# One written list of operations, engines and PSUM banks in place of a planner with priorities

## The chip, the cores and the metric

The kernel runs on one core of one Trainium2 chip. The metric is the device time of one execution in microseconds (us). Three runs of the kernel before took 1002.0, 1002.21 and 1002.55 us; the median, 1002.21, is its time.

## What is computed

Three stages follow one another. The first is a linear attention with a delta rule over 4 x 8 heads, 768 steps, head size 48; the other two are two-layer MLPs with 384 -> 2048 -> 384 features over the 3072 tokens that result.

```python
for t in range(S):                       # attention, k normalised first
    y[:, :, t] = einsum('bhd,bhde->bhe', q[:, :, t], state)
    v_old = einsum('bhde,bhd->bhe', state, k_n[:, :, t])
    state = state + beta_t * outer(k_t, v_t - v_old)
x = y.transpose(0, 2, 1, 3).reshape(3072, 384)
h = x @ w_in                             # first MLP
x = where(h >= 1, h, where(h <= -1, 0, (h + 1)**2 / 4)) @ w_out
h = x @ w_in2                            # second MLP
out = (h * clip(h + 3, 0, 6) / 6) @ w_out2
```

## The kernel before

**Attention in chunks.** The 768 steps are cut into 12 chunks of 64, named c0 to c11. For each chunk k and q are loaded and transposed (lines 904 to 922), the norms of k are worked out (`norms`, L862), the products k k and k q are formed on PE (`products`, L932), read out of PSUM and masked (L956, L964, L978). `inverse` (L993) then solves a triangular system. Its inner part is a chain of pairs, a multiplication (L1019) and a subtraction (L1024), each of which needs the one before; chunks c0 and c1 do it on DVE, c2 and later ones on POOL. DVE prepares it (L1040, L1046, L1048) and transposes the result (L1057, L1058), and small tiled matmuls on PE finish it. `chain` (L1123) subtracts the old values from V (L1137), multiplies by the solved matrix, forms the new state, and `chain_y` (L1174) writes the output as the MLP's input XB (L1245).

**MLPs.** Each fp32 product is made of three faster ones, from a high part and a low remainder of either operand. So every weight tile f (16 of 128 hidden columns per MLP) is loaded into RAWL or RAWR and split by `wload` (L1266): bit operations (L1303, L1306, L1309), a rounded copy for the high part (L715, L718), and a subtraction for the low part (L707). H means the first product, O the second; H1 b0 f3 is the first product of MLP 1, block 0, tile 3. Blocks 0 and 1 are one chunk each (256 tokens), the others two. A group of such a product is three matmuls. Between H and O the activation runs on ACT and DVE (L1372 to L1374), its result is split the same way (GH, GL). The second MLP starts when the attention and the first one are through.

**Who sets the order.** The functions above don't issue anything. They register operations in a `Plan` (`op`, L300): what it reads and writes, which engines may run it (`alts`, with an assumed duration for each) and a priority. `emit` (L331) then simulates all engines on the host, step by step, with these durations, priorities per kind and chunk (`PR`), a model of the clock and of PE's instruction fetch, and chooses each operation's engine, place and PSUM bank. While PE would have nothing to do it puts in a filler, a dummy matmul whose result nobody reads (`fill`, L1657), to keep the clock up; there are 40 of them, without dependence or on a converted weight. After that `rearrange` (L580) puts single operations elsewhere by a table `MOVES` and sets some engines by a table `TAKEN`, and `run` (L601) calls the functions in the final order. Each engine executes its own instructions in that order, and semaphores are set between them.

```python
        self.order = order
        self.rearrange()
        self.run()
```

Nearly all matmuls come from one helper line, L749; L707, L715, L718, L720 and L723 are helper lines as well (two-operand pass; copies on POOL, on ACT and on DVE; scaled copy on DVE). L771, L773 and L778 are the scalings by a per-partition factor.

Of the kernel before, what the change touches and what calls it, by code (L numbers as in the profile page):

```python
# [17 lines left out]
TAIL = dict(pe=235, dve=125, act=130, pool=45)  # L18
MLP = 50
RATIO = 0.649  # L20
NSMALL = 2
WINDOW = 4096 / 1.2
WARM, COLD = 0.39, 0.49
PR = dict(tl=67.962086, tp=0.420514, pk=1,
          pg={(0, 'chain'): -0.2539, (0, 'inv'): 3.364608, (0, 'kv'): 1.465035, (0, 'lv'): -4.010662, (0, 'norm'): -0.274261, (0, 'sv'): 1.013448,
# [5 lines left out]
              (2, 'chain'): -0.290685, (2, 'inv'): -0.035632, (2, 'kv'): 0.669398, (2, 'lv'): -2.096759, (2, 'norm'): -0.160388,  # L31
# [10 lines left out]
              (9, 'norm'): 0.012878, (9, 'pm'): -0.418629, (9, 'tok'): -0.040633, (9, 'y'): 1.271522}, dx=1.008178, sx=39.637984, dl=760.706049,  # L42
          ms=('act', 'dve'), wd=4, fm=9792.35537, aw=('act', 'dve', 'pool'), mg=8, fl=4694.34542, off=(-10.25393, 8.909221, -35.984542, -41.02295),
          mb=(80.821727, -28.998599), slots=2, fast=(0,), slate=0, mk=0, hm=-109.564616, kv=-31.465847, tok=-1.884445, norm=17.151989, tr=-1.768853,
          prod=-34.319006, pm=-5.471625, inv=-15.779498, sv=25.627625, w=-1.449, chain=8.008585, y=3.551141, wl=12.667074, wls=0.825794,
          mp=-10.624354, lv=-23.102311, first=-4.800254, bias=-1265.49322, fill=3000, tpool=(2, 3, 4, 5, 6, 7, 8, 9, 10, 11), hc=1, halves=1,
          biasa=1240.32542, b16=(0, 1, 2, 3), hyst=2858.41045, fgap=480.938837, me=100, c3=('act', 'dve'), back=2155.50193, dh=200,
          margin=845.586248, umargin=89.653885, urg=('inv', 's', 'u', 'y'), sw=(217, 95), ad=('act', 'dve'), dp=('dve', 'pool'), ct=4,
          dg=('dve', 'pool'), dw=('dve', 'pool'), pq=190)

MOVES = ((12, -1), (17, 1), (11, 17), (20, 21), (0, 20), (55, 4), (82, 55), (2, 38), (6, 2), (7, 6), (5, 39), (81, 5), (56, 19), (8, 41), (9, 8),
# [224 lines left out]
class Bank:  # L276
# [8 lines left out]
    def free(self, e):  # L285
        return 0.0 if self.last[0] in (None, e) else self.last[1]


class Plan:

# [316 lines left out]
def fused_kernel(  # L607
# [19 lines left out]
    CH = 64  # L627
# [1082 lines left out]
```

## Time and profile before

| | |
|---|---|
| Time, median of 3 runs | 1002.21 us (1002.0 to 1002.55) |
| Profiled execution, first to last instruction (span) | 1004.1 us |
| Its distance from the median | 1.9 us |
| Instructions | 27311 |
| PE busy | 967.3 us, 96% |
| DVE busy | 610.3 us, 61% |
| ACT busy | 480.9 us, 48% |
| POOL busy | 295.5 us, 29% |
| Chain that ended last, share of PE | 86% |

The page gives no other time of the profiled execution than its span, from the first to the last instruction, so the span stands for it.

A busy share is a mean over the whole span, and this kernel has parts with different limits: in the page's 40 slices PE is busy for 6 to 8 tenths in the first four and for 9 or more in nearly all others. A row of the view by stretches shows for each engine how long it was busy and how many instructions it ran, then the granted clock of PE as a share of the full one and the busy share of the DMA engines. A row of the groups has the line, the engine, the operation, the tiles (out<-in), the shapes and the count, then the busy time of all, the mean of one in ns, and the idle time before them. DVE's neighbouring instructions overlap by some hundredths of a us, so a sum of their durations can exceed the time that they cover.

### The profile page before, as it was taken

How to read it: one execution, taken by the hardware profiler on the slowest of the kernel's cores; microseconds unless marked ns; L12 is line 12 of the kernel's file. 1: busy time of each engine (PE TensorE's matmuls, PEld its weight loads, DVE VectorE, ACT ScalarE, POOL GpSimd, SP SyncE). 2: the span in 40 equal slices, each digit the busy share in tenths (PEclk: the TensorE clock that was granted, in tenths of full speed). 3: DMA queues.
4: the chain of work that ended last, by engine and by line, in shares of the span. 5: the costliest groups of instructions: out<-in, count | busy, mean ns of one | idle time of the engine just before them, and what ended most of it. 6: DMA issues, size and time to landing. Idle time of an engine off the chain costs nothing.

```text
span 1004.1 us, 27311 instructions
## 1 busy us (share of the span) xinstructions
PE 967.3 (96%) x11543; PEld 835.6 (83%) x11543; DVE 610.3 (61%) x1136; ACT 480.9 (48%) x897; POOL 295.5 (29%) x649
## 2 busy tenths in 40 slices
PE   6778799999999999999999999999999999999998
PEld 4667699878778787787887888998989898999998
DVE  5898798777887688777546886225242324242421
ACT  4877565556564564545445774224242323232422
POOL 2101641767558565585710222110000000000000
PEclk9678999999999999999999999999999999999999
DMA  8872442443333234222213664002200200200000
GB/s 158 202 199 63 112 91 42 91 71 56 52 86 58 34 59 100 33 45 73 80 42 94 211 206 138 13 1 84 74 32 1 64 32 16 66 14 1 32 2 31
DMA packets 208459, 71.77 MB, mean 71 GB/s; under 512 B 154960, under 2 KB 204240, under 8 KB 208336
## 3 DMA queue, kind: packets, MB, share of 16 engines
q1 hardware_dynamic: 205376, 69.44, 28.9%
q8 instruction: 90, 1.47, 0.6%
q10 hardware_dynamic: 2960, 0.59, 0.3%
q14 instruction: 33, 0.27, 0.1%
HBM read 53.68 MB, written 14.16 MB: 68 GB/s over the span
## 4 chain that ended last, share of the span: by engine, by line
PE 86%; DVE 2%; POOL 1%; ACT 1%; issue 0%; POOLq 0%
PE bank L749 86%; POOL TMP L1019 1%; POOL TL L1024 1%; DVE GF L1374 0%; ACT GF L1373 0%; ACT GF L1372 0%; DVE LT L778 0%; DVE X L956 0%; DVE KQ L978 0%; ACT GH L718 0%; DVE DL L1040 0%; DVE DL L1057 0%; DVE E L1137 0%; DVE SM L874 0%; ACT X L771 0%
## 5 line engine op out<-in xcount | busy, mean ns | idle before, releaser
L749 PE MATMUL bank<-XB,WLA 128*128 128x512 f32 (+1 forms) x1404 | 325.6, 379 | 2.9 <-DVE GF L1374 2.8
L749 PEld LDWEIGHTS bank<-XB,WLA 128*128 128x128 f32 x1404 | 249.9, 190 | 51.2 <-DVE GF L1374 6.0
L1378 DVE SCALAR_TENSOR_TENSOR GF<-GF,bank 128x512 f32<-128x512 f32 x96 | 65.7, 687 | 161.7 <-ACT GF L1377 161.7
L1377 ACT ACTIVATE GF<-bank 128x512 f32<-128x512 f32 x96 | 57.0, 598 | 166.3 <-PE bank L749 156.8
L1019 POOL TENSOR_TENSOR TMP<-TL,DL 128x126 f32<-128x126 f32 (+25 forms) x278 | 115.3, 415 | 62.5 <-DVE DL L1077 35.5
L749 PE MATMUL bank<-GH,WLA 128*128 128x512 f32 (+1 forms) x504 | 120.9, 367 | 0.2 <-ACT XB L718 0.2
L1024 POOL TENSOR_TENSOR TL<-TL,TMP 128x126 f32<-128x126 f32 (+25 forms) x278 | 113.3, 407 | 21.8
L749 PE MATMUL bank<-XB,WLB 128*128 128x512 f32 (+1 forms) x468 | 108.7, 377 | 0.0
L718 ACT ACTIVATE GH<-GF 128x512 fp32r<-128x512 f32 x106 | 66.7, 630 | 81.7 <-DVE GF L1374 30.8
L707 DVE TENSOR_TENSOR GL<-GF,GH 128x512 fp32r<-128x512 f32 x105 | 77.6, 739 | 35.6 <-ACT GH L718 26.5
L749 PEld LDWEIGHTS bank<-GH,WLA 128*128 128x128 f32 x504 | 86.4, 190 | 15.2 <-ACT XB L718 0.4
L749 PEld LDWEIGHTS bank<-XB,WLB 128*128 128x128 f32 x468 | 82.9, 188 | 15.5 <-DVE GF L1374 0.4
L1372 ACT ACTIVATE GF<-bank 128x512 f32<-128x512 f32 x96 | 56.9, 593 | 73.6 <-PE bank L749 69.1
L1374 DVE SCALAR_TENSOR_TENSOR GF<-bank,GF 128x512 f32<-128x512 f32 x96 | 65.7, 685 | 36.5 <-ACT GF L1373 35.9
L749 PE MATMUL bank<-GL,WLA 128*128 128x512 f32 (+1 forms) x252 | 64.8, 366 | 0.0
L1373 ACT ACTIVATE GF<-GF 128x512 f32<-128x512 f32 x96 | 60.5, 630 | 2.5
L749 PEld LDWEIGHTS bank<-GL,WLA 128*128 128x128 f32 x252 | 43.9, 190 | 7.4
L749 PE MATMUL bank<-WLA,GH 128*128 128x384 f32 x205 | 43.4, 350 | 0.0
L707 POOL TENSOR_TENSOR GL<-GF,GH 128x512 fp32r<-128x512 f32 x15 | 20.2, 1344 | 72.4 <-ACT GH L718 48.9
L749 PE MATMUL bank<-GH,WLB 128*128 128x512 f32 (+1 forms) x168 | 39.4, 362 | 0.0
L749 PEld LDWEIGHTS bank<-WLA,GH 128*128 128x128 f32 x205 | 38.0, 196 | 1.5
L964 ACT ACTIVATE KQ<-bank 64x256 f32<-64x256 f32 (+1 forms) x72 | 27.2, 380 | 21.9 <-PE bank L749 17.1
(197 smaller groups left out, 1440.7 us busy)
## 6 DMA issues: line engine op xcount, KB each, us to landing
XB<-X SPq DMA_DIRECT2D x36, 256.0 KB, 4.6
X<-XB SPq DMA_DIRECT2D x30, 256.0 KB, 2.6
KQ<-in_moe_w_out_dram SPq DMA_DIRECT2D x16, 384.0 KB, 4.2
KQ<-in_moe_w_in_dram SPq DMA_DIRECT2D x16, 384.0 KB, 4.5
KN<-in_k_dram SPq DMA_DIRECT2D x24, 192.0 KB, 3.9
RAWL<-in_moe_w_out_dram SPq DMA_DIRECT2D x12, 384.0 KB, 4.5
out_dram<-E SPq DMA_DIRECT2D x24, 192.0 KB, 1.9
RAWL<-in_moe_w_in_dram SPq DMA_DIRECT2D x24, 144.0 KB, 4.3
```

What stands on the lines that cost most here:

```text
L707: alts[e] = (d, lambda e=e: ENG[e].tensor_tensor(out=val(out), in0=val(in0), in1=val(in1), op=op))
L718: lambda: nc.scalar.activation(out=val(out), in_=val(in_), func=AF.Copy, scale=scale))
L749: nc.tensor.matmul(o, l, r, start=start, stop=stop, skip_group_check=skip)
L964: alts = {"act": (285, lambda o=o, pin=pin: nc.scalar.activation(out=o, in_=pin(), func=AF.Copy, scale=1.0))}
L1019: P.op(te, d, lambda t=t, s=s, r0=r0, a0=a0, a1=a1, m=m: ve.tensor_tensor(out=t[:, a0:a1], in0=TL[:, r0 + a0:r0 + a1, s:s + 1].to_broadcas ...
L1024: P.op(te, d, lambda t=t, s=s, r0=r0, a0=a0, a1=a1: ve.tensor_tensor(out=TL[:, r0 + a0:r0 + a1, 0:s], in0=TL[:, r0 + a0:r0 + a1, 0:s], in1 ...
L1372: P.op("act", da, lambda: nc.scalar.activation(out=gf, in_=ps, func=AF.Relu, scale=0.5, bias=0.5), r=hkeys(hb, hv), w=gk, prio=mp)
L1373: P.op("act", da + 48, lambda: nc.scalar.activation(out=gf, in_=gf, func=AF.Square), w=gk, r=gk, prio=mp)
L1374: P.op("dve", 1.06 * n + 60, lambda: nc.vector.scalar_tensor_tensor(out=gf, in0=ps, scalar=1.0, in1=gf, op0=ALU.max, op1=ALU.min), r=hkeys ...
L1377: P.op("act", da, lambda: nc.scalar.activation(out=gf, in_=ps, func=AF.Relu, scale=1.0 / 6.0, bias=0.5), r=hkeys(hb, hv), w=gk, prio=mp)
L1378: P.op("dve", 1.06 * n + 60, lambda: nc.vector.scalar_tensor_tensor(out=gf, in0=gf, scalar=1.0, in1=ps, op0=ALU.min, op1=ALU.mult), r=hkey ...
```

## The change

The planner goes: `emit`, `rearrange`, the tables `PR`, `MOVES` and `TAKEN`, all priorities, and the bookkeeping of banks. A text `ORDER` takes their place, with one word for each of the 4625 operations and each filler. `1005p` would be operation 1005 on POOL (a ACT, d DVE, p POOL, n none), `403b25` an operation that gets PSUM banks 2 and 5, `f` a filler, `f1.0` one that reads a converted weight. The new `run` goes through it, refuses an operation ahead of what it depends on, and calls the functions. Operations are numbered in the order of registration, which is the same in both.

```diff
+ORDER = """
...
+"""
...
-    def emit(self, banks, spare, fill):
...
-    def rearrange(self):
...
+    def run(self, banks, fill):
+        done = set()
+        for x in ORDER.split():
+            if x[0] == "f":
+                fill(tuple(map(int, x[1:].split("."))) if x[1:] else None)
+                continue
+            n, e, bs = re.fullmatch(r"(\d+)([adpn]?)(?:b(\d+))?", x).groups()
+            i = int(n)
+            o = self.ops[i]
+            if not o["deps"] <= done:
+                raise ValueError(f"operation {i} before {sorted(o['deps'] - done)}")
+            done.add(i)
+            for b, j in zip(o["alloc"], bs or ()):
+                b.tile = banks[int(j)]
             if o["dyn"] is not None:
                 o["alts"] = o["dyn"]()
...
+            if e:
+                o["eng"] = dict(a="act", d="dve", p="pool", n="none")[e]
+            o["alts"][o["eng"]][1]()
+        assert len(done) == len(self.ops)
...
-        P.emit(banks[5:8], banks[0:5], fill)
+        P.run(banks, fill)
```

Set side by side with the order that the planner before arrives at, the list has the same operations, and these differences:

- 83 operations run on another engine: 32 go from DVE to POOL, 23 from ACT to DVE, 13 from DVE to ACT, 8 from ACT to POOL, 3 each from POOL to ACT and to DVE, and one mask (409) is no instruction any more, since its read-out, now on DVE, multiplies by the mask itself. From DVE to POOL go the low parts of weight tiles f0 to f11 (L707), the masks of c0 to c3 (L978), scalings of V (L707) and low parts of activations; from ACT to POOL go the rounded copies of f4 to f9 and of two single pieces.
- 8 fillers are left of 40, all ahead of the product that makes c0's new state.
- Within PE 66 operations, within DVE and ACT 88 each, within SP 92 and within POOL 14 stand elsewhere relative to the others. Chunk 0's loads of v are issued after the first weight tiles instead of before; the loads of q for c3 later; on ACT's queue the mask and beta go ahead of the identity. In the products of c0 the second half comes before the first. The norms of c1 are mixed into c0's solve.
- The banks come from all eight from the start, where the planner gave the front banks 5 to 7 first.
- Behind H1 b1 f5 on PE (141.22 us in the profile before), and behind places between 138.4 and 141.3 us on the other engines, the order of every engine is the same in both.

## Rows read from the trace of the kernel before

**Rows 1.** The page: the span, and each engine's busy time.
```profile
span 1004.1 us, 27311 instructions
...
PE 967.3 (96%) x11543; PEld 835.6 (83%) x11543; DVE 610.3 (61%) x1136; ACT 480.9 (48%) x897; POOL 295.5 (29%) x649
```

**Rows 2.** Busy time by stretches: engine (instructions), clock share, DMA share, GB/s.
```profile
8.00:101.00 93.00, 73.46 (x1625) 63.12 (x1623) 81.37 (x217) 66.90 (x132) 11.71 (x17) 0.80 0.66 155
101.00:126.00 25.00, 18.94 (x601) 17.48 (x601) 19.14 (x35) 13.19 (x23) 15.70 (x34) 1.00 0.48 116
126.00:545.00 419.00, 417.61 (x7038) 343.62 (x7038) 321.75 (x608) 233.31 (x475) 237.00 (x561) 1.00 0.32 64
```

**Rows 3.** The chain that ended last: start us, us, what.
```profile
101.36 0.23 POOL TMP L1019
...
115.33 0.24 POOL TL L1024
...
125.94 52.43 PE bank L749 x1162
...
545.11 455.60 PE bank L749 x2268
```

**Rows 4.** DVE's groups by line and shape from 8 to 101 us.
```profile
L707 DVE TENSOR_TENSOR WLA<-RAWL,WLA 128x768 fp32r<-128x768 f32 x8 | 7.6, 950 | 0.0
L978 DVE TENSOR_TENSOR KQ<-KQ,MSK 128x256 f32<-128x256 f32 x12 | 4.9, 412 | 3.0 <-ACT KQ L964 3.0
...
L707 DVE TENSOR_TENSOR WLA<-RAWL,WLA 128x384 fp32r<-128x384 f32 x6 | 3.7, 621 | 1.2 <-ACT WLA L718 1.2
...
L1054 DVE TENSOR_SCALAR TL<-TL,PAR 128x256 f32<-128x256 f32 x4 | 1.4, 352 | 0.1
...
L720 DVE COPY KQ<-bank 112x512 f32<-112x512 f32 x2 | 1.4, 688 | 0.0
...
L707 DVE TENSOR_TENSOR E<-E,NT 128x384 f32<-128x384 f32 x2 | 1.1, 550 | 0.0
```

**Rows 5.** POOL's groups by line and shape from 8 to 135 us.
```profile
L707 POOL TENSOR_TENSOR WLA<-RAWL,WLA 128x384 fp32r<-128x384 f32 x2 | 2.1, 1039 | 9.4 <-ACT WLA L718 9.3
L715 POOL CAST WLA<-RAWL 128x768 fp32r<-128x768 f32 x2 | 1.9, 947 | 3.4 <-DVE RAWL L1309 3.4
L707 POOL TENSOR_TENSOR WLB<-RAWR,WLB 128x768 fp32r<-128x768 f32 x1 | 1.9, 1852 | 2.7 <-ACT WLB L718 2.7
```

**Rows 6.** DVE's groups from 551 to 587 us, where POOL splits weights too.
```profile
L707 DVE TENSOR_TENSOR WLA<-KQ,WLA 128x768 fp32r<-128x768 f32 x7 | 7.8, 1114 | 0.1
```

**Rows 7.** POOL in order of time from 550 to 590 us: start, us, what.
```profile
582.72 2.58 POOL L707 TENSOR_TENSOR WLA<-KQ,WLA 128x768 fp32r<-128x768 f32 x1
```

**Rows 8.** PE in order of time, several stretches: start, us, what [idle before <-releaser].
```profile
25.72 5.03 PE L749 MATMUL bank<-GH 128*128 128x512 f32 x14
...
39.77 1.11 PE L749 MATMUL bank<-DL,NH 32*32 32x32 f32 x65
...
88.60 1.48 PE L749 MATMUL bank<-XB,WLA 128*128 128x256 f32 x6
...
114.94 2.35 PE L749 MATMUL bank<-XB,WLA 128*128 128x256 f32 x18
119.07 1.30 PE L749 MATMUL bank<-NH,LT 32*32 32x32 f32 x128 [1.79 <-DVE NH L1058]
```

**Rows 9.** Busy time by stretches of 20 us.
```profile
40.00:60.00 20.00, 16.11 (x501) 13.46 (x491) 18.11 (x48) 17.46 (x38) 4.07 (x5) 0.59 0.68 179
60.00:80.00 20.00, 15.83 (x267) 14.60 (x268) 19.56 (x49) 16.11 (x24) 0.66 (x2) 0.83 0.95 239
```

**Rows 10.** SP's issues in order of time from 56 to 80 us.
```profile
63.04 2.24 SPq L1286 DMA_DIRECT2D RAWL<-in_moe_w_in_dram  x3
```

**Rows 11.** DMA issues from 0 to 100 us: count, KB each, median us to landing.
```profile
RAWL<-in_moe_w_in_dram SPq DMA_DIRECT2D x24, 144.0 KB, 4.3
```

**Rows 12.** DVE in order of time from 62 to 72 us.
```profile
71.91 0.56 DVE L1303 TENSOR_SCALAR TBS<-RAWL 128x768 int32<-128x768 int32 x1
```

More of the change, by code (lines that the diff above doesn't have):

```diff
@@ L316, in op @@
         alloc = (alloc,) if isinstance(alloc, Bank) else tuple(alloc)
-        us = list(uses) + list(alloc)
-        for b in us:
-            b.users += 1
-        self.ops.append(dict(eng=eng, dur=dur, fn=fn, deps=deps, prio=prio, alloc=alloc, uses=us, nbytes=nbytes, own=own, crit=crit, tag=self.tag,
-                             alts=alts or {eng: (dur, fn)}, dyn=dyn, load=load, port=port, tiled=tiled, q=q, urgent=urgent, bulk=bulk, extra=extra or {}, ni=ni, conv=conv))
-        return i
-    def dma(self, fn, ndesc, nbytes, **kw):
-        run = nbytes / ndesc
-        kw.setdefault("prio", 0.0)
-        cost = kw.pop("cost", None) or nbytes * max(1.0, 400.0 / run) / 360.0
-        return self.op(kw.pop("eng", "sp"), kw.pop("si", 475 + (155 if ndesc >= 512 else 0)), fn, nbytes=cost * 360.0, **kw)
@@ L331, in emit @@
-    def emit(self, banks, spare, fill):
-        ops = self.ops
-        n = len(ops)
-        succ = [[] for _ in range(n)]
-        left = [0] * n
-        ready = [0.0] * n
-        for i, o in enumerate(ops):
-            left[i] = len(o["deps"])
-            for d in o["deps"]:
-                succ[d].append(i)
-        avail = {}
-        def offer(i):
-            o = ops[i]
+        self.ops.append(dict(eng=eng, dur=dur, fn=fn, deps=deps, alloc=alloc, uses=list(uses) + list(alloc), tag=self.tag, alts=alts or {eng: (dur, fn)},
+                             dyn=dyn, tiled=tiled, ni=ni, dma=dma))
@@ L348, in offer @@
             if o["dyn"] is not None:
                 o["alts"] = o["dyn"]()
-            for e in o["alts"]:
-                avail[e].append(i)
-        for o in ops:
-            for e in list(o["alts"]) + ["none"]:
-                avail.setdefault(e, [])
-        for i in range(n):
-            if left[i] == 0:
-                offer(i)
-        free = {e: 0.0 for e in avail}
-        free["sp"] = 700.0
-        tiles = list(banks) + list(spare)
-        nb = len(banks)
-        bank_free = [0.0] * len(tiles)
@@ L383, in emit @@
-        tiled = False
-        quad = {}
-        pages = {}
-        moved = []
-        at = [0]
-        def blocked(t, dur):
-            end = t + dur
-            for x in reversed(moved[-6:]):
-                if t < x + 1050.0 and end > x:
-                    end = max(end, x + 1450.0)
-            return end - t
-        def late(n_, t, dur):
-            j, left_, x = (at[0] - 193) // 256 + 1, n_, 0.0
-            b = 256 * j + 193 - at[0]
-            while b < n_:
-                x += max(0.0, pages.get(j, 0.0) - (t + dur * b / n_ + x))
-                j += 1
-                b += 256
-            return x
@@ L576, in emit @@
-        self.order = order
-        self.rearrange()
-        self.run()
-    def rearrange(self):
-        ops, order = self.ops, self.order
-        for e, xs in TAKEN.items():
-            for x in xs:
-                o = ops[x]
-                o["eng"] = e
-                o["dur"], o["fn"] = o["alts"][e]
-        gone = {x for x, _ in MOVES}
-        nxt = {}
-        kept = [-1] + [x for x in order if x not in gone]
-        for a, b in zip(kept, kept[1:]):
-            nxt[a] = b
-        for x, after in MOVES:
-            nxt[after], nxt[x] = x, nxt.get(after)
-        order.clear()
-        x = nxt[-1]
-        while x is not None:
-            order.append(x)
-            x = nxt.get(x)
@@ L601, in run @@
-    def run(self):
-        for i in self.order:
-            self.ops[i]["fn"]()
+            if e:
+                o["eng"] = dict(a="act", d="dve", p="pool", n="none")[e]
+            o["alts"][o["eng"]][1]()
+        assert len(done) == len(self.ops)
 @with_exitstack
@@ L689, in fused_kernel @@
     P = Plan()
-    def pri(c, name):
-        return c + PR[name] - (PR["first"] if c == 0 else 0) + (PR["off"][c] if c < len(PR["off"]) else 0) + PR["pg"].get((c, name), 0)
     ENG = dict(dve=nc.vector, pool=nc.gpsimd)
-    def qd(sb_=None, ps=None, out=0):
-        return tuple(None if x is None else (x.start if isinstance(x, slice) else x) // 32 for x in (sb_, ps, out))
     def val(x):
@@ L707, in ttalt, with cpalt @@
             alts[e] = (d, lambda e=e: ENG[e].tensor_tensor(out=val(out), in0=val(in0), in1=val(in1), op=op))
-        return P.op(None, 0, None, alts=alts, port=("dve", "pool"), **kw)
-    def cpalt(engs, n, out, in_, ps, scale=1.0, more=0, **kw):
+        return P.op(None, 0, None, alts=alts, **kw)
+    def cpalt(engs, n, out, in_, ps, scale=1.0, **kw):
         alts = {}
@@ L813, in load_blocks @@
                     dst = STB[p0:p0 + 32, :, th, 0:n]
-                    P.dma(lambda ap=ap, dst=dst: nc.sync.dma_start(out=dst, in_=ap), 32 * U, 32 * U * 4 * n,
-                          si=490, w=[("stb", dl, f, th)], pre=[("st", i, b) for i in range(2) for b in range(2)], prio=pri(c, "tok"), bulk=True)
+                    P.dma(lambda ap=ap, dst=dst: nc.sync.dma_start(out=dst, in_=ap), 32 * U, 32 * U * 4 * n, w=[("stb", dl, f, th)], pre=[("st", i, b) for i in range(2) for b in range(2)])
     def block_transposes(c):
@@ L1124, in chain @@
         st = c % 2
-        pr = pri(c, "chain")
         P.tag = f"chain c{c}"
@@ L1175, in chain_y @@
         st = c % 2
[L1176 to L1177 removed]
         blk, tau = divmod(c, 2)
         xi = blk % 2
[L1180 removed]
+        fast = c == 0
         bys = [Bank(), Bank()]
@@ L1322, in fused_kernel @@
     OB2 = [5, 6, 7, 0]
-    MP = PR["mp"]
-    owned = set()
-    def own(bs):
-        new = [3 + b for b in bs if b not in owned]
-        owned.update(bs)
-        return new
     def slot(hbs, ng, n):
@@ L1398, in pe @@
                         mm(banks[OB1[j]][:, o0:o0 + n], wl(f, wh, DM + j * 128, DM + (j + 1) * 128), gt(), start=first, stop=last, skip=blk < NSMALL)
-                P.op("pe", KT * (n * 0.4276 + 8.3), pe, ni=2 * KT, r=rk, w=[k_ for b in OB1 for k_ in hkeys(b, ov)], prio=MLP, own=own(OB1))
+                P.op("pe", KT * (n * 0.4276 + 8.3), pe, ni=2 * KT, r=rk, w=[k_ for b in OB1 for k_ in hkeys(b, ov)])
             else:
@@ L1552, in fused_kernel @@
         front(c + 1)
-    steps1 = [(0, f) for f in range(PR["mg"])]
+    steps1 = [(0, f) for f in range(MG)]
     for i in range(0, NF, 2):
-        steps1 += [(1, i), (1, i + 1)] + [(0, PR["mg"] + j) for j in (i, i + 1) if PR["mg"] + j < NF]
+        steps1 += [(1, i), (1, i + 1)] + [(0, MG + j) for j in (i, i + 1) if MG + j < NF]
     todo1 = []
```

670 lines of the change are left out of this document (302 added, 368 removed), and 232 rows, old and new, of tables (MOVES, pg).

## The prediction

> **What bounds the kernel now.** The page gives the span and the busy time of each engine [rows 1]: PE is busy for 967.3 of 1004.1 us, so at most some 37 us of idle PE can be won, plus whatever PE does at less than full speed. The busy time by stretch [rows 2] says where: from 126 us on PE is busy for 417.6 of 419 us at full clock. The loss lies ahead of that. From 8 to 101 us PE has 73.5 of 93 us at a mean granted clock of 0.80, and DVE has 81.4 of 93: counted piece by piece in its queue, with the overlaps of neighbours, DVE hardly stands still. From 101 to 126 us both idle for about a quarter.
>
> The chain of waits [rows 3] names the same places. From 125.94 us to the end it is PE with a few short steps between, the last 455.60 us in one piece. Before that it runs over DVE (L1040 to L1048, the set-up of chunk 2's solve), then from 101.36 to 115.57 us over POOL's alternating L1019 and L1024, and back over DVE to PE, which stood still 1.79 us for it at 119.07 [rows 8]. So an edit is worth what it takes from DVE's queue ahead of 101 us, and what it lets PE do while the solve runs. An edit behind 126 us could only lose.
>
> **What the list changes, and where it stops.** I set the written list beside the order, engines and banks that the planner of the kernel before arrives at. Behind H1 of block 1, f 5 (near 141 us) PE, DVE, ACT, POOL and SP each have the same order in both. All changes lie in the first seventh, so the sum has to be made there, and PE must carry it to the end. That the planner's code goes is work on the host and costs nothing.
>
> *DVE's queue ahead of chunk 2's solve* (the L1048 that releases the POOL step at 101.36). 38 pieces leave: 8 weight subtractions of 768 columns, 8 x 0.950 = 7.6; 6 of 384, 6 x 0.621 = 3.7; 9 masks (8 go to POOL, 1 is merged into a bank's read-out), 9 x 0.412 = 3.7; 3 scalings of V, 3 x 0.55 = 1.7; 12 others by their own durations 5.3, two transposes' read-outs of 0.688 the largest, 3 of them only put later: 22.0 us [rows 4]. 22 pieces come: 5 scalings of 256 columns at 0.352 = 1.8; 6 copies of weights 2.5; the squares of chunk 0, priced as a two-operand pass of 768 columns, 0.95; four small copies 1.0; a transposed bank's read-out 0.69; two of chunk 1's reads pulled ahead 1.05; three others 0.8: 8.8 us. **Term 1: -13.2 us.**
>
> *POOL, where most of it lands.* It has 11.7 us of work in those 93 us [rows 2]. It gets 8 x 1.85, 6 copies of 0.947 and a smaller one, 6 x 1.04 [rows 5], and 11 smaller ones that I estimate at 0.7 to 1.5 each, scaled from these by their columns (9 to 10 us), less 4 that it gives up: some 33 us more, so 45 of 93. It has room, and the cover is its idle time; without it each 768-column subtraction would cost twice what DVE paid. The Trainium skill says so as a rule (GPSIMD Engine Reference, Engine selection): elementwise work on two inputs belongs on VectorE, GpSimd being about 2x slower. Rows 4 and 5 agree (0.95 against 1.85), and by the rule alone this change would be a mistake; the trace's answer is that this engine was idle.
>
> *What POOL's work costs DVE beside it.* Where POOL and DVE both work on SBUF, DVE's subtraction of 768 columns takes 1.114 us in the mean against 0.950 [rows 4, 6], 17% more, and POOL's own up to 2.58 [rows 7]. In the new list POOL is active for half of the stretch, and DVE has 68 us of work left in it. Reading PSUM should not be touched, SBUF work should: between nothing and 17% of all 68 us, 0 to 11.6. I take 4.0, a third of the upper end, since only half of the time overlaps and part of that reads PSUM. **Term 2: +4.0.**
>
> *Fillers.* 40 dummy matmuls become 8. The 14 from 25.72 us on took 5.03 us [rows 8], and they lie in PE's waits, so taking them out gives nothing by itself. They do bear on the clock: a solve's product of 128 small matmuls takes 1.30 us at full clock, and 1.11 for half of them, 2.2 in all, at 1.2 GHz [rows 8]. In 40 to 60 us the clock was 0.59 with fillers running [rows 9], so most of chunk 0's steps ran at the low level anyway; one of the two large products of chunk 0 loses its full clock. **Term 3: +1.0** (0 to 6 if all six tiled steps there lost it).
>
> *Waits that take the place.* DVE freed by 13 us will stand for somebody: POOL's last subtraction (1.85) now sits in front of the solve's first step in POOL's own queue, and the L1024s wait for it. On ACT 31 pieces leave and 16 come in the whole changed part, none of them long. On SP the loads are only reordered: chunk 0's v goes behind the first weights, chunk 1's k and q ahead; the count of DMAs is the same. On ACT's queue the mask goes ahead of the identity, half a microsecond for the first transpose, and the other half's k comes earlier; I count both at nothing, because what leaves and comes on DVE before chunk 0's solve ends is level too. Bank numbers move no instruction; a bank not yet read out would show as PE waiting, up to the 2 to 3 us of its longest waits, but all eight banks are now open to the front. **Term 4: +2.2**, near one POOL subtraction of 1.85; from nothing to 5, two of the slowest (2.58, [rows 7]).
>
> At chunk 2's solve that makes -13.2 + 4.0 + 1.0 + 2.2 = -6.0 us.
>
> *From there to PE's full run.* POOL's solve stays 14.2 us and starts 6.0 earlier. PE waits behind it at 119.07. The new list has put ten more groups of the MLP and one transpose before that product; a group of three costs 2.35/6 = 0.39 [rows 8], so 4 us of work that stood behind the wait fits ahead of it, in time that PE idled (6 of 25 us, [rows 2]). I give 1 us back for products of chunks 2 and 3 that then come before DVE is ready. **Term 5: -3.0.**
>
> **Sum: -9.0 us.** From the profiled 1004.1 that is 995.1; the runs shown have a median of 1002.21, 1.9 under the profiled span, so I predict **993.2 us**. A measurement of this kernel can tell about 0.2%, 2 us, from no change.
>
> **Rivals.**
>
> *The whole DVE gain comes through.* If terms 2 to 4 are near nothing, -13.2 - 3.0 = -16.2: 986. For it: the overlaps in DVE's queue; against it: rows 6.
>
> *Weights hold the front.* DMA is 0.95 busy from 60 to 80 us [rows 9]. The last piece of block f8 is in the SP row at 63.04, lands some 4.3 us after its issue [rows 10, 11], near 68.3, and DVE starts on it at 71.91 [rows 12]: 3.6 us of room. If transfers cannot come earlier, DVE gains no more than that while f7 to f10 are converted, and the sum is -3.6 with nothing from term 5: 998.6. Against it: SP's list moves f7 forward by 5 to 17 places and most of f8 by up to 5, and f11, the last one that the solve waits behind, has more room.
>
> *It is given back later.* Between 126 and 545 us the common order waits for DVE or POOL as much as PE came early: 1002.2. Against it: DVE is busy for 321.8 and POOL for 237.0 of 419 us [rows 2], so both can catch up.
>
> *Slower: the clock.* With 8 fillers PE goes into the MLP cold and stays at 1.2 GHz. Two groups then take 1.48 us [rows 8], 0.74 each against 0.39: +0.35. Some 68 groups stand ahead of 126 us, +24 us, and twelve tiled steps there at +0.9 make +11; PE's idle time from 60 to 126 us is about 15 us (4.2 to 80 us and 6.1 from 101 us on, [rows 2, 9], between them taken like the first). It decides as soon as more than 15 of these 35 us are paid; three quarters of them, the more likely form, give 26 - 15 = +11: 1013. For it: the row at 88.60 is half speed in the middle of MLP work, after a stall. Against it: from 100 us on the clock was full at two thirds busy. The Trainium skill (TensorE: Matmul & The Clock Gate, Part 1) says that activity releases the clock and that idling throttles it, which speaks against leaving fillers out; by it the front's products would all be cold, term 3 at its upper end and the sum -4.
>
> **Chances.** The forecast 0.52 (988 to 997.5), the full gain 0.13, the weights 0.17, given back 0.08, the clock 0.10 with any other way to be slower. Faster than 1000.2: 0.82; within 0.2%: 0.08; slower: 0.10. The range from 984 to 1001.5 takes in the full gain and the weights, and leaves out the slower case and most of the no-change case; the forecast's own range is 988 to 997.5.
>
> **What would show it.** In the profile after: POOL busy for 40 to 50 us of the first 95 and DVE's share still above 0.85; the first L1019 on POOL at 95 to 96 instead of 101.36, and the PE piece that stands at 125.94 some 9 us earlier; L1303 and L707 on DVE longer where POOL is active; from there to the end the same length as before within 1 us. Wrong would be: the chain passing over a DMA landing between 60 and 90 us, POOL's L707 as what the solve waits for by more than 3 us, a granted clock under 0.7 from 60 to 110, or new idle time of PE between 126 and 545.

## The result, and the profile after

The changed kernel took 1013.3 us (median of 4 runs, 1012.75 to 1014.3), the kernel before 1002.38 (4 runs, 1002.0 to 1003.3). The ratio on record is 1.009, with a 95% interval of 1.0071 to 1.0109; the two medians alone give 1.0109, its upper end. Forecast were 993.2 us, in a range of 984 to 1001.5. By the ratio it is 9 us slower (10.9 by the medians) where 9 us faster were expected, and outside the range.

The two profiled executions are 7.2 us apart, not 10.9. In every run of these two kernels whose span is known the time is 1.7 to 1.9 us above the span, so the profiled execution of before (span 1004.1) belongs to a time near 1005.9, longer than any of the runs behind 1002.38. The experiments below ran on four chips, on which the same kernel before had medians of 1005.0 to 1006.5; so each is given as a ratio to the kernel before, run beside it. Two executions, one of pool_back_near (1880.53 us, the one that was traced) and one of the kernel before (1562.93 us), were far longer than all others and count in no ratio.

The page after, the lines that answer to [rows 1]:

```profile
span 1011.3 us, 27274 instructions
...
PE 960.4 (95%) x11511; PEld 830.0 (82%) x11511; DVE 622.4 (62%) x1116; ACT 472.4 (47%) x883; POOL 331.7 (33%) x683
```

The same stretches as in [rows 2] (PE, weight loads, DVE, ACT, POOL, clock, DMA share, GB/s):

```profile
8.00:101.00 93.00, 59.09 (x1505) 50.33 (x1505) 83.68 (x190) 55.76 (x113) 39.13 (x40) 0.80 0.66 155
101.00:126.00 25.00, 22.42 (x435) 20.96 (x435) 21.60 (x33) 17.06 (x29) 18.82 (x37) 0.93 0.39 84
126.00:545.00 419.00, 415.63 (x7266) 343.14 (x7267) 323.73 (x609) 230.18 (x471) 242.81 (x570) 1.00 0.33 64
```

POOL did take the work: 39.1 us instead of 11.7 ahead of 101 us. DVE should have become freer by 13 us and is busy 2.3 us longer, with 27 instructions fewer. PE lost 14.4 us of work in that stretch at the same mean clock of 0.80, and behind 126 us all is as before. The chain of waits, with the rows that answer to [rows 3]:

```profile
110.83 0.87 POOL TMP L645
...
127.55 1.32 PE bank L383 x81
...
595.52 412.39 PE bank L383 x2079
```

L645 and L650 are the old L1019 and L1024. Chunk 2's solve on POOL starts at 110.83 instead of 101.36, 9.5 us later where 6 us earlier were forecast. From there to the last common place (H1 of block 1, f 5) it is 36.9 us instead of 39.9, and from that to the end 863.6 instead of 862.9. So the whole miss lies ahead of that solve, in DVE's queue. There are two causes. The first is to be seen in DVE's and POOL's instructions in order of time:

```profile
62.28 1.90 DVE L645 TENSOR_TENSOR TMP<-TL,DL 128x63 f32<-128x63 f32 x1
...
64.97 0.21 DVE L650 TENSOR_TENSOR TL<-TL,TMP 128x63 f32<-128x63 f32 x1
...
66.24 1.78 DVE L650 TENSOR_TENSOR TL<-TL,TMP 128x60 f32<-128x60 f32 x1
...
68.73 0.56 DVE L868 TENSOR_TENSOR XB<-bank,XB 128x384 fp32r<-128x384 f32 x1
```

```profile
62.24 1.86 POOL L345 TENSOR_TENSOR WLA<-RAWL,WLA 128x768 fp32r<-128x768 f32 x1
...
66.08 1.86 POOL L345 TENSOR_TENSOR WLA<-RAWL,WLA 128x768 fp32r<-128x768 f32 x1
...
77.78 1.88 POOL L345 TENSOR_TENSOR WLA<-RAWL,WLA 128x768 fp32r<-128x768 f32 x1
...
84.40 1.84 POOL L345 TENSOR_TENSOR WLA<-RAWL,WLA 128x768 fp32r<-128x768 f32 x1
...
90.15 2.15 POOL L345 TENSOR_TENSOR WLA<-RAWL,WLA 128x768 fp32r<-128x768 f32 x1
```

A step of chunk 1's solve on DVE takes 0.21 us by itself and 1.90 and 1.78 us when POOL's subtraction began shortly before it: it ends 0.1 us after POOL's. It isn't slowed in proportion to its size, it stands still until POOL is through. More of DVE, beside the last three of POOL's subtractions shown:

```profile
77.97 1.98 DVE L412 SCALAR_TENSOR_TENSOR LT<-X,PAR,LT 128x256 f32<-128x256 f32 x1
...
81.34 0.94 DVE L505 TENSOR_REDUCE SM<-X 128x16 f32<-128x768 f32 x1
...
84.45 1.82 DVE L511 TENSOR_TENSOR SM<-SM 128x16 f32<-128x16 f32 x1
...
90.50 1.83 DVE L516 TENSOR_TENSOR ND<-SM,BT 128x16 f32<-128x16 f32 x1
```

L511 and L516 work on 16 columns and take 0.17 us alone. What doesn't wait is told by the same rows: L868 above reads a PSUM bank and took its usual 0.56 us though POOL worked from 68.58 to 69.41, the reduction at 81.34 took 0.94 beside POOL's copy (81.48 to 82.36), and the transposes from SBUF (1.07 and 0.71 us) are not longer either. Taken over all 178 instructions that DVE has ahead of the solve in both kernels, the excess is 19.8 us, and all of it falls on instructions that one of POOL's overlaps; the others are together no longer than before.

The second cause is at the very start, on ACT (after, then before):

```profile
7.77 1.28 ACT L389 ACT_TABLE_LOAD   x1 [7.77 <-DMA G<-in_k_dram]
...
9.06 0.63 ACT L389 ACTIVATE GH<-GF 128x512 fp32r<-128x512 f32 x1
9.71 1.28 ACT L388 ACT_TABLE_LOAD   x1
11.00 0.20 ACT L388 ACTIVATE SM<-GF 128x1 f32<-128x1 f32 x1
```

```profile
3.00 1.28 ACT L754 ACT_TABLE_LOAD   x1 [3.00 <-POOL ST L760]
4.29 0.20 ACT L754 ACTIVATE SM<-GF 128x1 f32<-128x1 f32 x1
```

The list puts a copy (L389) ahead of the first square root (L388, in the kernel before L754), and both behind ACT's DMA issues. Before, one table load lay in idle time at 3.00 and served both. Now the copy loads a table and the root another, and the root's buffer is what the norms write into next:

```profile
11.24 0.95 DVE L505 TENSOR_REDUCE SM<-X 128x16 f32<-128x768 f32 x1 [2.82 <-ACT SM L388]
```

DVE waits 2.82 us there; before, the same reduction ran at 8.60:

```profile
8.60 0.95 DVE L874 TENSOR_REDUCE SM<-X 128x16 f32<-128x768 f32 x1 [8.60 <-ACT X L868]
```

### The profile page after: what moved, and what is told of

Same layout as the page of the kernel before. It is cut to its first block, busy times and chain, and to the rows that moved or that the text cites. A ratio compares the mean times of both kernels' runs of the same rounds, so it can differ in the third digit from the quotient of the medians.

```text
span 1011.3 us, 27274 instructions
## 1 busy us (share of the span) xinstructions
PE 960.4 (95%) x11511; PEld 830.0 (82%) x11511; DVE 622.4 (62%) x1116; ACT 472.4 (47%) x883; POOL 331.7 (33%) x683
## 4 chain that ended last, share of the span: by engine, by line
PE 82%; DVE 4%; DMA 3%; SPq 3%; POOL 3%; issue 2%; ACT 2%; DVEq 0%; POOLq 0%; ACTq 0%
PE bank L383 82%; SPq L909 1%; DMA RAWL<-in_moe_w_in_dram 1%; POOL WLA L345 1%; SPq L434 1%; DMA E<-in_v_dram 1%; DMA KQ<-in_moe_w_out_dram 1%; SPq L488 1%; POOL TMP L645 1%; POOL TL L650 1%; DVE GF L987 1%; DVE TBS L926 0%; ACT GF L985 0%; DMA KN<-in_k_dram 0%; DMA G<-in_k_dram 0%
## 5 line engine op out<-in xcount | busy, mean ns | idle before, releaser
L645 POOL TENSOR_TENSOR TMP<-TL,DL 128x126 f32<-128x126 f32 (+25 forms) x278 | 114.0, 410 | 58.1 <-DVE DL L703 35.5
L650 POOL TENSOR_TENSOR TL<-TL,TMP 128x126 f32<-128x126 f32 (+25 forms) x278 | 112.9, 406 | 21.8
L383 PE MATMUL bank<-WLA,GH 128*128 128x384 f32 x194 | 39.3, 340 | 4.3 <-ACT KQ L356 4.3
L383 PEld LDWEIGHTS bank<-WLA,GH 128*128 128x128 f32 x194 | 34.8, 189 | 5.8 <-ACT KQ L356 4.7
```

The source lines that it names most:

```text
L383: nc.tensor.matmul(o, l, r, start=start, stop=stop, skip_group_check=skip)
L645: P.op(te, d, lambda t=t, s=s, r0=r0, a0=a0, a1=a1, m=m: ve.tensor_tensor(out=t[:, a0:a1], in0=TL[:, r0 + a0:r0 + a1, s:s + 1].to_broadcas ...
L650: P.op(te, d, lambda t=t, s=s, r0=r0, a0=a0, a1=a1: ve.tensor_tensor(out=TL[:, r0 + a0:r0 + a1, 0:s], in0=TL[:, r0 + a0:r0 + a1, 0:s], in1 ...
```

## The experiments

Each kernel is the list with some words changed, in two cases with some lines of code besides. 1.009 is the number to explain. Each line of the table is a ratio to the kernel before on the same chip.

| kernel | ratio | 95% interval |
|---|---|---|
| changed kernel | 1.0090 | 1.0071 to 1.0109 |
| pool_alone: old order, 40 pieces on POOL | 1.0076 | 1.0054 to 1.0097 |
| fill8_alone: old order, 8 fillers | 1.0009 | 0.9994 to 1.0025 |
| pool_useless: old order, useless POOL passes | 1.0044 | 1.0029 to 1.0060 |
| pool_split: new list, shorter POOL instructions | 1.0055 | 1.0038 to 1.0071 |
| pool_back, pool_back_near: new list, pieces back | 1.0207, 1.0204 | 1.0186 to 1.0228, 1.0185 to 1.0224 |
| pool_back_timed: the same at other places | 1.0046 | 1.0031 to 1.0060 |
| start_alone_undone: new list, old start | 1.0051 | 1.0033 to 1.0070 |
| pool_back_start: both undone | 1.0008 | 0.9996 to 1.0020 |
| no_late_filler | 1.0077 | 1.0060 to 1.0093 |
| quiet_solve, quiet_solve2 | 0.9993, 1.0005 | 0.9980 to 1.0005, 0.9989 to 1.0020 |
| best_of_both | 1.0002 | 0.9987 to 1.0018 |

**The kernel before as a list.** 

> The kernel before, with its own order, engines, banks and 40 fillers written out as a list: no instruction differs. Every theory expects the time of the kernel before, 1002.4 us within 1. It shows in addition whether the profiled execution of before (1004.1 us from first to last instruction) was a typical one: the four executions of the changed kernel had spans 1.7 to 1.9 us below their times, so a typical span of before would be near 1000.6 us, and then the 7.2 us between the two traces become about 10.7.

Measured: 0.9994 (0.9977 to 1.0012). The written form costs nothing measurable. The profiled execution had a span of 1003.3 us, and the 23 runs of before beside it spread from 1002.7 to 1009.6 us: a difference of a few us between two single traces shows nothing by itself. The 9.5 us at chunk 2's solve are more than that: in five traces without POOL's new pieces in the old order it starts at 98.5 to 102.7 us, in three with them, uncut, in the new list at 108.6 to 110.9.

**POOL's pieces alone.** In the old order, 40 words such as

```diff
-157d 175d 222a 223d
+157p 175p 222p 223p
```

> The kernel before with one part of the change alone: the same 40 pieces (32 from DVE, 8 from ACT) run on POOL, at the places that they have in the old order; fillers, loads and all other engines as before. By the prediction's terms DVE loses 17.0 us ahead of chunk 2's solve and pays 4 for working beside POOL: 13 us earlier there and about 990 us. Theory A: each POOL pass holds up DVE's passes on SBUF, some 40 per cent of POOL's 38.5 new us and more are paid back, 16 to 22 us, so DVE gains nothing or loses up to 5 us and the time is 1001 to 1007. Theories B and C: POOL's work is harmless, so 990 to 996 as predicted.

Measured: 1.0076, 7.6 us slower where the prediction's terms wanted it faster. DVE's share ahead of 101 us hardly moved, with POOL at 46.7:

```profile
8.00:101.00 93.00, 68.95 (x1542) 59.14 (x1541) 80.60 (x184) 57.88 (x117) 46.65 (x48) 0.82 0.66 155
```

17.0 us of work left DVE and the common instructions got 17.3 us longer. The 16 to 22 expected of theory A hold; 4 of the prediction don't. Theory A's time, 1001 to 1007 and so at most 5 us slower, was passed. In the old order this part alone costs 7.6 us; taken out of the new list it gives 4.4 (below). What makes the two differ was not followed; the solve starts at 106.27 here, so 4.9 of the 6.1 us between this trace and that of before lie ahead of it.

**The fillers alone.** 32 words `f` go from the old order. 

> The kernel before with another part alone: 8 fillers instead of 40, ahead of the same products as in the new list. Theory A: the fillers bear on little, 1002.4 within 1.5 (some of chunk 0's products at half speed, +1 us by the prediction's term 3, most of it in PE's waits). Theory B: most of the 11 us, 1008 to 1013, with a granted clock of 0.5 to 0.7 from 20 to 80 us. Theory C: no change.

Measured: 1.0009, no measurable change. The clock did fall, to 0.58 from 20 to 40 us (0.81 before):

```profile
20.00:40.00 20.00, 13.16 (x251) 9.53 (x252) 17.63 (x61) 12.05 (x27) 1.80 (x4) 0.58 0.90 203
```

The products there lie in PE's waits. Theory B is out as the cause: the forecast's slower rival named the right time, 1013, and the wrong mechanism.

**Useless work on POOL.**

```diff
             o["alts"][o["eng"]][1]()
+            if i in DUP:
+                self.dup(i)
...
+    def dup(i):
+        n = 768 if i > 210 else 384
+        s = RAWR.bitcast(F32)
+        nc.gpsimd.tensor_tensor(out=s[:, 0:n], in0=s[:, 768:768 + n], in1=s[:, 768:768 + n], op=ALU.subtract)
```

> The kernel before, all its work on its old engines, and in addition 10 useless subtractions on POOL (6 of 384 and 4 of 768 columns, on a staging buffer that is not yet in use, so the program does more than asked for and computes the same). Nobody waits for them. Theory A (while POOL runs a pass on SBUF, DVE's passes on SBUF stand still): 6 x 1.04 + 4 x 1.85 = 13.6 us of POOL beside a full DVE, most of it is added to DVE's instructions ahead of chunk 2's solve, 8 to 13 us, and the time rises by 7 to 12 us. Theory D (what hurt was the lateness of POOL's results, twice DVE's duration in a chain of five passes, and pieces that wait in POOL's queue): no result is late here, so the time stays within 1.5 us.

Measured: 1.0044, 4.4 us slower, below the 7 to 12 of theory A and clear of theory D. The ten passes took 12.7 us on POOL and DVE's instructions ahead of the solve got 6.2 us longer: about half of a pass is caught, not most of it. POOL, then DVE beside it:

```profile
54.68 7.24 POOL L1297 TENSOR_TENSOR RAWR<-RAWR 128x768 f32<-128x768 f32 x4
```

```profile
57.08 1.68 DVE L692 SCALAR_TENSOR_TENSOR DL<-DL,PAR 128x256 f32<-128x256 f32 x1
58.80 1.32 DVE L663 TENSOR_TENSOR TMP<-TL,DL 128x15 f32<-128x15 f32 x1
...
60.52 1.43 DVE L668 TENSOR_TENSOR TL<-TL,TMP 128x15 f32<-128x15 f32 x1
```

Work that nobody waits for lengthens DVE steps of 0.17 us (128x15) to 1.3 and 1.4. So it is not lateness of POOL's results.

**Shorter POOL instructions.**

```diff
-            alts[e] = (d, lambda e=e: ENG[e].tensor_tensor(out=val(out), in0=val(in0), in1=val(in1), op=op))
+            alts[e] = (d, lambda e=e: [ENG[e].tensor_tensor(out=x, in0=y, in1=z, op=op) for x, y, z in zip(*map(pieces, (out, in0, in1)))])
```

Here `pieces` cuts an operand into runs of 192 columns for the weight passes on POOL. 

> The changed kernel with the weight passes on POOL (22 moved ones and 4 older ones) cut into pieces of 192 columns, one instruction each; nothing else changes. Theory A in its strict form (the one that starts first holds the access until its instruction ends): DVE gets in after 0.3 to 0.6 us and no longer after 1.9, so the excess of 19.8 us on the common DVE instructions falls to 10 to 15 and the time by 3 to 8 us. Rival (the two share a bandwidth): the excess stays at 19 to 21 us and the time is the same or 1 us more, for the added instructions.

Measured: 1.0055 against 1.0090, some 3.5 us faster, the two intervals just touching. DVE's excess fell from 19.8 to 13.5 us, inside the 10 to 15 expected, and no instruction waited more than 1.0 us. The price is on POOL:

```profile
L353 POOL TENSOR_TENSOR WLA<-RAWL,WLA 128x192 fp32r<-128x192 f32 x48 | 35.8, 779 | 3.8 <-DVE WLA L366 3.1 <-ACT WLA L364 0.6
...
L353 POOL TENSOR_TENSOR WLB<-RAWR,WLB 128x192 fp32r<-128x192 f32 x4 | 2.3, 606 | 0.0
```

A quarter of a subtraction now takes 0.78 us in the mean, four 3.1 where the whole took 1.94 in the changed kernel. Most of that is the quarters' own length, since the shortest take 0.6 and four of those 2.4; the rest is waiting, with single quarters of up to 1.34 us: the two engines take turns by the instruction. That speaks for a hold of one whole instruction, and against a shared bandwidth.

**Undoing it in the new list, twice wrongly.** First the 40 pieces on their old engines at the list's places:

```diff
-193p 410p 222p 223p 495p 496p
+193d 410d 222a 223d 495d 496d
```

> The changed kernel with one part undone: the 32 pieces that went from DVE to POOL and the 8 rounded copies that went from ACT to POOL run on their old engines again, at the places that the new list gives them; all else of the list stays. Theory A (a DVE pass on SBUF stands still while POOL runs one): the 19.8 us by which the common DVE instructions ahead of chunk 2's solve got longer and 3.7 us of the new ones go, 16.8 us of returned work come, so that solve starts some 7 us earlier than 110.8, at 103 to 105, and the time falls by about 7, to 1006 (1003 to 1008). Theory B (the missing fillers and the clock): nothing of the loss hangs on POOL; the time stays at 1013 within 2 or rises, DVE being fuller. Theory C (the new order of the start: 2.6 us later norms, loads, fillers that wait): 1011 to 1013.

> The changed kernel with 36 of the 40 pieces back on DVE and ACT, and each put right behind the last operation that it depends on, so that none stands in DVE's queue behind a wait that was meant for others; the four scalings of V, which wait for late loads, stay on POOL. Theory A: some 15 us of work come back to DVE and 20 us or more of standing still go, so it is faster than the changed kernel by 3 to 9 us. Rival (the rest of the list, its late loads and its fillers, is what costs, as the first undoing seemed to say): no faster than the changed kernel, or slower by up to 13 us as there.

Measured: 1.0207 and 1.0204, far from theory A's forecast; it looked as if POOL's help were what saved the new list. The trace of the first shows another thing, DVE in order of time:

```profile
70.85 0.56 DVE L345 TENSOR_TENSOR E<-E,ND 128x384 f32<-128x384 f32 x1 [2.27 <-issue]
77.68 0.56 DVE L345 TENSOR_TENSOR E<-E,NT 128x384 f32<-128x384 f32 x1 [6.26 <-DMA E<-in_v_dram]
```

and SP, which issues nothing between 57.3 and 65.98 us:

```profile
56.70 0.61 SPq L488 DMA_DIRECT2D E<-in_v_dram  x1
65.98 0.35 SPq L909 DMA_DIRECT2D RAWL<-in_moe_w_out_dram  x1
```

DVE's excess is 1.2 us, as theory A wants, but it stands idle for 32.9 us ahead of the solve instead of 16.9. A scaling of V that waits on POOL for its load harms nobody; in DVE's queue everything stands behind it. A place in a list is good for the engine that the list gave it. In the second undoing each subtraction stood directly behind the copy that it needs; in its one trace, of the execution of 1880.53 us, DVE's idle time ahead of the solve was 33 us again, but that trace can carry little, and its single waits were not followed.

**Undoing it at POOL's own times.** 

> A third undoing of the POOL moves in the changed kernel, since both earlier ones put new waits into DVE's queue (33 us of standing idle ahead of chunk 2's solve, against 17 in the changed kernel): 36 pieces back on DVE and ACT, each at the place in DVE's or ACT's order at which the trace of the changed kernel shows POOL starting on it, the subtraction 0.4 us behind its copy; the scalings of V stay on POOL. Theory A alone (what costs is DVE standing still beside POOL): 3 to 9 us faster than the changed kernel. Theory A with the rest of the list being worse than the old order: as slow as the changed kernel or slower by up to 12 us, with DVE's excess near nothing and its idle time above 17 us, and then the list was fitted to POOL's help and is bad without it.

Measured: 1.0046 against 1.0090, 4.4 us faster than the changed kernel. DVE's excess is 1.2 us, its idle time 19.1, and the solve starts at 104.80 instead of 110.83:

```profile
104.80 0.80 POOL L645 TENSOR_TENSOR TMP<-TL,DL 128x15 f32<-128x15 f32 x1 [8.35 <-DVE DL L674]
```

Half of the loss is left, and it is there already at 35 us, where chunk 0's solve on DVE ends (35.2 us, 32.0 before).

**The start of ACT's queue.** The first eleven entries as before, and POOL's memset that they need first:

```diff
-13 11 12 0 56 55 57 14 3 58 2
+12 11 0 55 2 56 57 3 58 13 14
```

> The third undoing (36 POOL pieces back at their times, ratio 1.0046) with the first eleven entries of ACT's queue, and POOL's first memset, in the order of the kernel before. In the changed kernel ACT loads its table and makes its first small value only at 9.7 to 11.2 us, behind its DMA issues, DVE stands 2.8 us before the norms, and chunk 0's solve on DVE ends at 35.2 us instead of 32. Theory C, as the cause of what is left: the 2.8 us of idle DVE go, chunk 0's solve ends at 32 to 33.5, and the time falls by 1 to 3 us, a ratio of 1.0015 to 1.0035. Rival: PE's products of chunk 0 wait for chunk 0's loads anyway (they start at 14.56), so nothing is gained and the ratio stays at 1.0046 within its interval.

Measured: 1.0008, down from 1.0046, 3.8 us, more than the 1 to 3 expected, and no longer different from the kernel before. Chunk 0's solve ends at 32.4 us. One table load, early again, and DVE's reduction 2.7 us sooner (ACT, then DVE):

```profile
2.99 1.28 ACT L388 ACT_TABLE_LOAD   x1 [2.99 <-POOL ST L394]
```

```profile
8.51 0.95 DVE L505 TENSOR_REDUCE SM<-X 128x16 f32<-128x768 f32 x1
```

> The changed kernel with only the start of ACT's queue (eleven entries) and POOL's first memset in the old order; all POOL pieces stay on POOL. It splits the loss of 9.0 us in the changed kernel the other way round. If the two causes add up, the start gives 3.8 us here as it did without the POOL pieces (ratio 1.0046 to 1.0008), and POOL's standing costs the 4 to 6 us that are left: ratio 1.004 to 1.006, with DVE's excess still at 19 to 21 us. If the start is hidden here, since DVE is late anyway: 1.008 to 1.009.

Measured: 1.0051, as expected if they add. The start is worth 3.9 us with POOL's pieces and 3.8 without, POOL's pieces 4.4 and 4.3. Together 8.2 of 9.0 us, and what is left (0.8 us, interval -0.4 to 2.0) is no change. Both runs put back the whole start of ACT's queue, the order of its DMA issues included; how much of the 3.8 us is the second table load, and how much the place of the root behind those issues, is not shown.

**The filler that waits.** The word `f0.0` ahead of `362b12` goes. 

> The changed kernel without one of its 8 fillers, the one ahead of the product that makes chunk 0's new state. It writes PSUM bank 4, which chunk 2's transposes had before, and ACT reads these out at 58.97 us: PE stood still from 54.71 to 59.02, though the product behind it had its inputs at 56.41. Theory A: PE's product comes 2.6 us earlier, but DVE is the one that is full there, so 0 to 1 us. Theory C (waits of this kind on PE are the loss): 2 to 3 us faster.

Measured: 1.0077, 1.3 us faster than the changed kernel with intervals that overlap; DVE's excess and the start of the solve (110.88) are as with it. The stall itself is real, PE with the filler and without:

```profile
59.02 0.69 PE L383 MATMUL bank<-WLA,GH 128*128 128x384 f32 x1 [4.32 <-ACT KQ L356]
```

```profile
56.17 0.40 PE L383 MATMUL bank<-E,KN 64*48 64x48 f32 x4 [1.27 <-DVE E L773]
```

The first row is the filler itself. Without it PE's product is through 2.9 us sooner (58.25 instead of 61.17) and hardly anything follows, as theory A had it, by which DVE is the one that is full.

**Tries for something faster.** The hold works the other way too. In the kernel before POOL's step of 128x48 took 1.07 us beside DVE's subtraction (POOL, then DVE), and the step of 128x48 that came later in the same solve 0.27:

```profile
104.19 1.07 POOL L1019 TENSOR_TENSOR TMP<-TL,DL 128x48 f32<-128x48 f32 x1
```

```profile
104.18 0.94 DVE L707 TENSOR_TENSOR WLB<-RAWR,WLB 128x768 fp32r<-128x768 f32 x1
```

```diff
-645d ... 646d ... 628d ... 736p
+628d 646d 645d ... 736d
```

> The kernel before with three pieces elsewhere: DVE's two scalings of V for chunk 2 behind the transposes that end chunk 2's solve, and one low part of an activation (the POOL pass of 1.30 us at 120.74, beside which a DVE pass of 0.48 took 1.56) on DVE. Theory A works both ways: POOL's L1019 at 106.96 took 1.06 us beside DVE's scaling and the like of it 0.31 alone; without it the solve ends 0.8 to 1.2 us earlier, and the step behind it 0.5 to 1.0: 0.5 to 2 us faster, at the limit of what can be measured. Rival (the solve's length is not set by DVE): no change or 0.5 us slower, as PE waits for the two scalings.

> A try for a kernel faster than both: the quieter solve of before (two scalings of V behind it, one low part on DVE) and, besides, chunk 2's four masks moved from DVE's queue ahead of that solve to DVE's idle places at 122 and 124 us; they are needed at 152. Three of them (0.42 + 0.40 + 0.44 us) stand directly ahead of the solve, so it should start 1.2 us earlier, and with the quieter solve the time falls by 1.5 to 2.5 us. If the solve is not what PE waits for, nothing changes.

Measured: 0.9993 and 1.0005. The solve did get shorter, from 14.2 us to 12.9 and 12.7; the time didn't move by anything measurable. Little was to be had, since PE has other work there and idled only 1.79 us for it [rows 8]. The earlier start that the second try was made for did not show: its solve starts at 102.74 us in the one trace.

> A try for a kernel faster than both, from the undone start and POOL (ratio 1.0008). There the whole front is 5 to 7 us ahead of the kernel before until 112 us, and then chunk 2's mask on DVE stands still for 2.06 us beside POOL's subtraction of f13 (1.87 us), with the end of chunk 2's solve behind it in DVE's queue, and PE waits 3.42 us. So: that subtraction behind the solve's last transposes, chunk 2's four masks 10 to 15 us later, one scaling of V and one low part on DVE behind the solve's own steps, and without the filler that waits for a bank. PE's product should come 1.9 us earlier and with the filler 2 to 3.5 us be gained: a ratio of 0.9970 to 0.9990. If something else is late there, 0.9995 to 1.001.

Measured: 1.0002. The place that it was made for behaves as expected. In pool_back_start DVE's mask stood behind POOL, and PE behind both (DVE, POOL, PE):

```profile
114.13 2.06 DVE L606 TENSOR_TENSOR KQ<-KQ,MSK 128x256 f32<-128x256 f32 x1
```

```profile
114.02 1.89 POOL L345 TENSOR_TENSOR WLB<-RAWR,WLB 128x768 fp32r<-128x768 f32 x1
```

```profile
118.42 1.35 PE L383 MATMUL bank<-NH,LT 32*32 32x32 f32 x128 [3.42 <-DVE NH L684]
```

In best_of_both PE waits 0.83 us there:

```profile
120.43 1.30 PE L383 MATMUL bank<-NH,LT 32*32 32x32 f32 x128 [0.83 <-POOL TL L658]
```

But the front was 3.7 us later in this execution (its solve starts at 103.99, at 100.31 in pool_back_start), with a clock of 0.50 from 20 to 60 us where pool_back_start had 0.60 and 0.55; whether the clock is the reason was not tested. No kernel tried is measurably faster than the one before.

## Why the prediction was wrong, step by step

The frame held: PE saturated behind 126 us, the common tail the same within 1 us (862.9 and 863.6 us), all to be decided in DVE's queue ahead of chunk 2's solve. Of the first 95 us POOL was busy for 40.6, at the lower end of the 40 to 50 announced, and DVE for a share of 0.83, just under the 0.85 (from 8 to 101 us it was 0.90). The sum for that queue went wrong in two terms.

DVE's queue by the two traces, up to the instruction that releases the solve: 38 pieces leave with 22.0 us, 22 come with 12.5, the 178 common ones take 19.8 more, idle time is 2.8 less, and neighbours overlap 2.0 less. That is +9.5 us.

**Term 1 (-13.2).** What leaves was read from the same rows both times, so its 22.0 us were no test. Of what comes, 8.8 was the undisturbed price and 12.5 the disturbed one.

**Term 2 (+4.0, bounds 0 to 11.6) is the step that failed.** It measured +19.8 on the common instructions, 1.7 times its upper bound of 11.6, and up to 3.7 more on the new ones. The mistake is in how the row was read: the means of one form, 1.114 against 0.950 us [rows 4, 6], were taken as a charge in proportion, 17% of DVE's own work, as if the two engines shared a bandwidth. They were a mixture: six of the seven passes took 0.95 or 0.96 us, and one, which began behind a pass of POOL, 2.07 (DVE, then POOL, in the kernel before):

```profile
576.40 0.95 DVE L707 TENSOR_TENSOR WLA<-KQ,WLA 128x768 fp32r<-128x768 f32 x1
...
581.50 2.07 DVE L707 TENSOR_TENSOR WLA<-KQ,WLA 128x768 fp32r<-128x768 f32 x1
```

```profile
581.46 1.30 POOL L707 TENSOR_TENSOR GL<-GF,GH 128x512 fp32r<-128x512 f32 x1 [2.08 <-DMA KQ<-in_moe_w_in_dram]
```

POOL's own 2.58 [rows 7], which the prediction saw, stood in the same way behind that DVE pass. A hold costs the rest of the *other* engine's instruction, whatever one's own length: 1.9 us on a step of 0.2. Its size is to be counted in POOL's time, not DVE's: pool_alone gives 17.3 us of excess for 38 us of added POOL work, pool_useless 6.2 for 12.7, both near half, and the changed kernel 19.8 to 23.5 for 33, 0.6 to 0.7. I take it that for the rest of the time DVE reads PSUM, transposes, reduces, stands idle or is ahead of POOL; that was not counted. Half of the 33 us that the prediction puts on POOL is 16.5 us; with it in place of 4.0 the sum at the solve would have been +6.5 instead of -6.0, and +3.5 at the end: slower, if by less than measured. The trace of before had such rows (581.50, and 104.19 further up), and the diff says it too: the planner that it removes keeps a `port` on these operations, and lets an operation of DVE or POOL that has one begin only when the last such operation is done:

```diff
-                    if e in o["port"]:
-                        t = max(t, port_free)
...
-            if e in o["port"]:
-                port_free = end
```

The Trainium skill (SBUF — State Buffer, section "SBUF: two separate sides") has the rule and I passed it by for the factor of two: the pair of ports that DVE and GpSimd share is "an exclusive lock, not a bandwidth split"; the one that starts first has it for the whole instruction, and on DVE's side it concerns passes in a two-port mode, and those with two SBUF inputs if GpSimd's instruction reads SBUF. The trace agrees, 1.90 us for a step of 0.21, and so do the forms that did not wait. Passes with one SBUF input waited too (in the changed kernel a TENSOR_SCALAR of 0.55 us took 1.91 at 95.40); in which mode they ran no trace shows.

**Term 4 (+2.2), in the part on ACT's queue "I count both at nothing"**, measured 3.8 to 3.9 us. I priced the swap of a mask and an identity load and did not look at which function comes first on ACT: 2.8 us of DVE idle, with a second table load in it. What the term did price, POOL's last subtraction ahead of the solve's first step, cost nothing: it ended at 110.07 us, and the step then waited 0.76 us more for DVE.

```profile
108.18 1.89 POOL L345 TENSOR_TENSOR WLA<-RAWL,WLA 128x768 fp32r<-128x768 f32 x1 [3.15 <-ACT WLA L356]
110.83 0.86 POOL L645 TENSOR_TENSOR TMP<-TL,DL 128x15 f32<-128x15 f32 x1 [0.76 <-DVE DL L674]
```

The cover that I named, "what leaves and comes on DVE before chunk 0's solve ends is level too", was true of the work and not of the time: that solve ended 3.3 us later. The Trainium skill (ScalarE: Activation LUTs, What ACT_TABLE_LOAD costs) gives about 1283 ns for one load; the rows show 1.28 us each.

**Term 3 (+1.0)** was about right: 1.0009 alone, which can't be told from nothing. **Term 5 (-3.0)** was met in its size: from the solve's first step to the last common place 39.9 us became 36.9. PE had 32.7 us of work there and 4.2 of idle time instead of 34.2 and 5.7, so about half of it is work done earlier and half idle time; no experiment took it apart.

**The rivals.** The time of the slower one, 1013, was met by accident: fill8_alone shows that the fillers don't make it. The weights were not what held the front: pool_alone, with the old loads in the old order, loses 7.6 us. Given back later is excluded by the tail. The rival that was missing is the rule of the hold; it would have ended slower.

## What to carry to other kernels

Before an elementwise pass goes to an idle POOL, look for single rows in which a short DVE pass on SBUF ends just after a POOL one: if there are any, POOL's idle time is not free, and about half to 0.7 of what it took on came back to a full DVE here. Put DVE's passes that read PSUM, and its transposes, beside it (not tried here), keep POOL's instructions short if they must run, and look at the few longest instances of a group and not at its mean. An order written for one set of engines isn't an undoing for another: when a piece goes back, place it by the times of the trace, or its waits land in a queue that can't afford them.

## What the runs showed that was not expected

- DVE's passes on SBUF stood still for the rest of a POOL instruction, up to 1.7 us beyond their own length; those that read PSUM, transposes and reductions did not. It works both ways: POOL's steps of 0.3 us took up to 1.07 beside a DVE pass of 0.94.
- Cutting POOL's instructions into quarters lowered DVE's excess from 19.8 to 13.5 us and made a subtraction on POOL 3.1 us long instead of 1.94, of which 2.4 is four times the shortest quarter.
- A copy ahead of the first square root on ACT made two table loads of 1.28 us; the root first made one, which served both.
- In the old order PE's mean clock from 20 to 40 us was 0.58 with 8 fillers and 0.81 with 40, in a stretch where PE waits for others, and the time did not move measurably (1.0009, 0.9994 to 1.0025). The changed kernel, with 8 as well, had 0.92 there and 0.50 from 40 to 60 us.
